# Retention and softplus feed-forward on one core: all attention in double steps of 64x64 products

## The chip, the core and the metric

The kernel runs on one core of one Trainium2 chip. Time is device time in microseconds, the median of repeated runs. The engines that matter are TensorE (PE, with its weight loads as PEld), VectorE (DVE), ScalarE (ACT), GpSimd (POOL) and SyncE (SP), which issues the DMAs.

## The reference

```python
scores = scale * np.matmul(q, k.transpose(0, 1, 3, 2))        # batch 8, heads 8, 576 positions, 64 dims
gamma = 1.0 - 2.0 ** (-5.0 - np.arange(H, dtype=np.float32))  # one decay for each head
Dmat = np.where(rel >= 0, gamma[:, None, None] ** rel[None, :, :], 0.0)
attn = np.matmul(scores * Dmat, v)                            # retention: causal, no softmax
x = attn.transpose(0, 2, 1, 3).reshape(B * S, H * D)          # 4608 tokens x 512
h = x @ w_in                                                  # 512 x 2048
g = np.maximum(h, 0.0) + np.log1p(np.exp(-np.abs(h)))         # softplus
out = g @ w_out                                               # 2048 x 512
```

All inputs and the output are float32; the weights `w_in` and `w_out` are read as 64-bit words.

## The kernel before

**Feed-forward.** The 4608 tokens form 9 units of 512. Each unit passes 16 slots, one for each 128 columns of the hidden layer: 144 slots. In slot i, `hidden_mm` (L391) makes 128 hidden features of 512 tokens with 12 products of 512 columns, and `output_mm` (L423) adds the slot before into four output banks with 12 more. Both use numbers split into a rounded head and a rest (`HI`, `LO`), three products for each exact one (`TERMS`). Between the two stand `logs` (three ACT operations, L399 to L401), `softplus` (DVE, L405) and `softplus_split` (ACT L409, DVE L410).

**Weights.** They come as 32 pieces of 512 KB, two for each slot of the first unit, through three staging buffers, and are converted in four parts: `weight_a` (ACT L455, DVE L457), `weight_b` (DVE L463), `weight_c` (ACT L471) and `weight_d` (DVE L476). Three pieces (`START_WEIGHTS`) are taken up before the first slot; slot i converts pieces 3 + 2i and 4 + 2i, and finishes the one before.

**Attention.** The tokens are also cut into 36 chunks of 128; there are 4 pairs of heads. Retention in chunks needs, for each head: scores k.q inside the chunk under a causal mask, the values times these scores, the state (the sum of k v over earlier chunks, decayed) times q, and the new state. A batch element is 4.5 chunks long, so it begins at the start or in the middle of a chunk (`_chunk_kind`): there a mask and a cleared part of k keep the two apart. There are two ways to do it:

- *Double steps*, for the first 9 chunks, 18 in all: two pairs of heads at once, in plain float32. Scores are 4 products with 64 rows and 128 columns (L163), the state 4 with 64 columns (L168), the values 4 of 128 rows into 64 outputs (L205), the state times q 4 of 64x64 with 128 columns (L211). Each such product appears as two PE records. In L211 both row groups of the array write to one PSUM bank. Nine double steps (`AHEAD`) run in an opening before the first slot, the others one in every second slot.
- *Split steps*, for the other 27 chunks, 108 in all, one in each slot from slot 19: one pair of heads, whose operands POOL scales (L252, L257), ACT and DVE split into head and rest (L266 to L268), and PE multiplies in 9 products of 256 columns (L277, L286, L359). Scores are added and masked and split again by ACT, DVE and POOL (L295 to L329), states likewise (L316 to L340). ACT and DVE write the result into the tokens (`value_out`, L372 and L376).

**Order.** It is written out by hand: each engine runs its instructions in the order of the program, and an instruction that waits holds what is behind it on its engine. All loads and stores are issued on SP's one queue: raw q, k, v of a step (`load_double` and `load_upto`), weights, constants and outputs. A load waits for its buffer. In an opening iteration m, the scores of step m come first on PE, then the values of step m - 1. In a slot, the attention's products stand ahead of the hidden product.

Of the kernel before, what the change touches and what calls it, by code (L numbers as in the profile page):

```python
# [23 lines left out]
NSTEP = NCHUNK * NPAIR  # L24
# [3 lines left out]
STEPS = CPU * NPAIR  # L28
# [3 lines left out]
PCHUNK = 9  # L32
NDOUBLE = PCHUNK * NPAIR // 2
AHEAD = STEPS // 2 + 1
NPLAIN = PCHUNK * NPAIR
LEAD = NPLAIN - 2 * (NDOUBLE - AHEAD) - 1
PIECE = 512
VCOLS = slice(3 * C, 4 * C)
START_WEIGHTS = 3
OPENING = 5  # L40
OPEN = (6 * C + H + NPAIR, 6 * C)
RAWS = 2
# [18 lines left out]
def retention_softplus_ffn(ctx: ExitStack, tc, opening, first, others, w, dec, vsc, gchp, out):  # L61
# [10 lines left out]
    ps_y = ctx.enter_context(tc.tile_pool(name="ps_y", bufs=1, space=PSUM, side="right"))  # L72
    ps_h = ctx.enter_context(tc.tile_pool(name="ps_h", bufs=2, space=PSUM, side="right"))


    plain_pools, weight_pools = ExitStack(), ExitStack()
    ps_att = plain_pools.enter_context(tc.tile_pool(name="ps_att", bufs=1, space=PSUM))
    rawp = plain_pools.enter_context(tc.tile_pool(name="rawp", bufs=2))
    pconst = plain_pools.enter_context(tc.tile_pool(name="pconst", bufs=1))
    wst = weight_pools.enter_context(tc.tile_pool(name="wst", bufs=WBUFS, side="right"))  # L80
    later = {}

    vsc_sb = const.tile([P, H], F32, name="vsc_sb")
    gchp_sb = const.tile([P, NPAIR], F32, name="gchp_sb")


    parts = [pconst.tile([P, n], F32, name=f"part{i}") for i, n in enumerate(OPEN)]
    decp_sb = [x[:, 4 * C:6 * C].rearrange("p (s c) -> p s c", s=2) for x in parts]
    vscp_sb = parts[0][:, 6 * C:6 * C + H]
    gchp0_sb = parts[0][:, 6 * C + H:6 * C + H + NPAIR]  # L90
    mask = pconst.tile([P, C], F32, name="mask")
    mask2 = pconst.tile([P, C], F32, name="mask2")
# [15 lines left out]
    def load_double(m):  # L108

        if m == 0:  # L110
            at = 0
            for x in parts:
                nc.sync.dma_start(x, opening[:, at:at + x.shape[1]])
                at += x.shape[1]
            kq, kv = (x[:, 0:4 * C] for x in parts)
        elif m == 5:
            kq, kv = (moe.tile([P, 4 * C], F32, tag="ab", name="raw_ab") for _ in range(2))
            for i, x in enumerate((kq, kv)):
                nc.sync.dma_start(x, first[m - 1][:, 4 * C * i:4 * C * (i + 1)])
        else:  # L120
            pool, tag = (moe, "g") if m in (3, 4, 8) else (rawp, "rawp")
            r = pool.tile([P, 8 * C], F32, tag=tag, name=f"raw_{tag}")
            nc.sync.dma_start(r, first[m - 1])
            kq, kv = r[:, 0:4 * C], r[:, 4 * C:8 * C]
        kq, kv = (x.rearrange("p (a s c) -> p a s c", a=2, s=2) for x in (kq, kv))
        live[-1 - m] = dict(k=kq[:, 0], q=kq[:, 1], kp=kv[:, 0], v=kv[:, 1])
# [3 lines left out]
    def scale_next():  # L130


        m = scaled[0]
        if -1 - m not in live:
            return
        scaled[0] += 1
        L = live[-1 - m]
        half = m % 2
        nc.gpsimd.tensor_mul(L["q"], L["q"], decp_sb[half])
        start = _chunk_kind(m // 2)[0]  # L140
        if start:
            nc.gpsimd.memset(L["kp"][0:start], 0.0)
        if m >= AHEAD:
            v, f = value_scale(m)
            nc.gpsimd.tensor_mul(v, v, f.unsqueeze(2).broadcast_to([P, 4, D]))

    def value_scale(m):
        return live[-1 - m]["v"].rearrange("p s (h d) -> p (s h) d", h=2), vscp_sb[:, 4 * (m % 2):4 * (m % 2) + 4]
# [8 lines left out]
    def scores_double(m, banks):  # L157

        L = live[-1 - m]
        for s in range(2):  # L160
            for h in range(2):
                rows = slice(h * D, (h + 1) * D)
                nc.tensor.matmul(banks[h][:, s * C:(s + 1) * C], L["k"][rows, s], L["q"][rows, s], start=True, stop=True)  # L163
        if _chunk_kind(m // 2)[1]:
            for s in range(2):
                for h in range(2):
                    rows = slice(h * D, (h + 1) * D)
                    nc.tensor.matmul(banks[0][rows, 2 * C + s * D:2 * C + (s + 1) * D], L["kp"][:, s, rows],  # L168
                                     L["v"][:, s, rows], start=True, stop=True, skip_group_check=True)
        L["banks"] = banks  # L170

    def scores_double_out(m):
        L = live[-1 - m]
        start, follows = _chunk_kind(m // 2)
        a = moe.tile([P, 2, 2, C], F32, tag="osb", name="a2")
        msk = mask2 if start else mask
        for h in range(2):
            nc.vector.tensor_mul(a[:, h], L["banks"][h][:, 0:2 * C].rearrange("p (s c) -> p s c", s=2),  # L178
                                 msk.unsqueeze(1).broadcast_to([P, 2, C]))
        L["a"] = a  # L180
        L["before"] = states.get(m % 2)
        states[m % 2] = None
        if follows:
            st = L["banks"][0][:, 2 * C:3 * C].rearrange("p (s d) -> p s d", s=2)
            s = att.tile([P, 2, D], F32, tag="s", name="s2", bufs=NPAIR + 1)
            if start is None:
                nc.vector.tensor_add(s, st, L["before"])
            else:
                nc.vector.tensor_copy(s, st)
            half = m % 2  # L190
            nc.gpsimd.tensor_mul(s, s, gchp0_sb[:, 2 * half:2 * half + 2].unsqueeze(2).broadcast_to([P, 2, D]))
            states[m % 2] = s

    def values_double(m, banks):

        L = live[-1 - m]
        start, _ = _chunk_kind(m // 2)
        n_cross = C if start is None else start
        if L["before"] is None:
            n_cross = 0  # L200
        o = [b[:, VCOLS] for b in banks]
        for s in range(2):
            for h in range(2):
                rows = slice(h * D, (h + 1) * D)
                nc.tensor.matmul(o[s][rows], L["v"][:, s, rows], L["a"][:, h, s], start=True,  # L205
                                 stop=not n_cross, skip_group_check=True)
        if n_cross:
            for s in range(2):
                for h in range(2):
                    rows = slice(h * D, (h + 1) * D)  # L210
                    nc.tensor.matmul(o[s][rows, 0:n_cross], L["before"][rows, s], L["q"][rows, s, 0:n_cross],  # L211
                                     start=False, stop=True, skip_group_check=True)
        L["o"] = o

    def values_double_out(m, both=None):
# [480 lines left out]
```

## Time and profile before

| | |
|---|---|
| median of 3 runs | 950.91 us (950.89 to 951.14) |
| profiled execution | 951.72 us, its span 950.0 us |
| mean granted TensorE clock | 0.999 |
| PE busy | 941.0 us, 99% of the span, 4946 records |
| DVE, ACT busy | 663.9 us (70%), 676.0 us (71%) |
| POOL busy | 274.8 us (29%) |
| bytes moved | 79.86 MB |

A PE record is busy from its start to a modelled end, and records overlap, so PE's share of 99% says that it always had something in hand, not that the array was full. The length of a piece of PE work is read from the start of one group to the start of the next. `x8` counts records; idle time in square brackets stands in front of the group and names what ended it.

### The profile page before, as it was taken

The numbers are of one execution on the slowest core, as the hardware profiler recorded it, in microseconds if no ns is written. First come the engines' busy times: TensorE is split into PE (matmuls) and PEld (weight loads), VectorE is DVE, ScalarE is ACT, GpSimd is POOL, SyncE is SP. The second block draws the span as 40 slices with busy tenths as digits, with TensorE's granted clock in tenths as the row PEclk, the third lists the DMA queues.
The fourth block names the chain that finished last, engine by engine and source line by source line (L and its number), as shares of the span: only waits on it lengthen the run. The fifth ranks groups of instructions, "written<-read, shape, count | busy, mean of one in ns | idle before, by whom it ended". The sixth has DMA issues, their size and how long they took to land.

```text
span 950.0 us, 14542 instructions
## 1 busy us (share of the span) xinstructions
PE 941.0 (99%) x4946; PEld 789.0 (83%) x4946; DVE 663.9 (70%) x1511; ACT 676.0 (71%) x1453; POOL 274.8 (29%) x497
## 2 busy tenths in 40 slices
PE   8999999999999999999999999999999999999998
PEld 6777778888888888888888888888888888888886
DVE  6777856777877787777777787777777777753222
ACT  7586756777777787777777787777777777764444
POOL 5111113333333332333343333233333333310000
PEclk9999999999999999999999999999999999999999
DMA  8666531222312222223212222223212222201001
GB/s 303 200 193 203 187 135 50 67 58 60 111 53 65 67 95 67 67 58 104 67 53 65 67 95 68 67 57 105 67 51 66 72 90 67 67 1 45 1 1 45
DMA packets 28730, 79.86 MB, mean 84 GB/s; under 512 B 3440, under 2 KB 3440, under 8 KB 28656
## 3 DMA queue, kind: packets, MB, share of 16 engines
q1 hardware_dynamic: 28656, 78.93, 26.6%
q8 instruction: 39, 0.64, 0.3%
q14 instruction: 35, 0.29, 0.1%
HBM read 69.48 MB, written 9.44 MB: 83 GB/s over the span
## 4 chain that ended last, share of the span: by engine, by line
PE 91%; ACT 4%; DVE 3%; DMA 1%; issue 1%; POOL 0%; DVEq 0%; ACTq 0%; POOLq 0%
PE h L391 39%; PE y L423 38%; PE os L359 6%; PE sc L277 3%; PE os L286 2%; DMA wst<-w 1%; DVE g L410 1%; DVE ab L405 1%; ACT w L471 1%; ACT ab L400 1%; ACT ab L401 1%; DVE wst L463 1%; DVE a L178 1%; ACT wst L455 1%; PE idle L512 0%
## 5 line engine op out<-in xcount | busy, mean ns | idle before, releaser
L391 PE MATMUL h<-xt,w 128*128 128x512 f32 (+1 forms) x1740 | 419.7, 390 | 1.2 <-DVE w L476 1.2
L423 PE MATMUL y<-w,g 128*128 128x512 f32 x1728 | 416.1, 390 | 0.6 <-DVE g L410 0.6
L423 PEld LDWEIGHTS y<-w,g 128*128 128x128 f32 x1728 | 323.9, 188 | 70.0 <-DVE g L410 2.9
L391 PEld LDWEIGHTS h<-xt,w 128*128 128x128 f32 x1740 | 317.6, 189 | 63.4 <-DVE w L476 2.7
L252 POOL TENSOR_TENSOR raw<-raw,dec_sb 128x256 f32<-128x256 f32 x108 | 96.4, 893 | 429.0 <-DMA raw<-others 381.2
L410 DVE TENSOR_TENSOR g<-ab,g 128x512 fp32r<-128x512 f32 (+1 forms) x145 | 103.4, 713 | 87.3 <-ACT g L409 86.2
L405 DVE SCALAR_TENSOR_TENSOR ab<-h,ab 128x512 f32<-128x512 f32 (+1 forms) x145 | 99.8, 688 | 90.1 <-ACT ab L401 87.5
L409 ACT CAST g<-ab 128x512 fp32r<-128x512 f32 (+1 forms) x145 | 89.5, 617 | 98.7 <-DVE ab L405 97.5
L399 ACT ACTIVATE ab<-h 128x512 f32<-128x512 f32 (+1 forms) x145 | 86.3, 595 | 72.0 <-PE h L391 72.0
L401 ACT ACTIVATE ab<-ab 128x512 f32<-128x512 f32 (+1 forms) x145 | 91.3, 630 | 4.7
L400 ACT ACTIVATE ab<-ab 128x512 f32<-128x512 f32 (+1 forms) x145 | 91.2, 629 | 4.6
L266 ACT CAST hl<-raw 128x768 fp32r<-128x768 f32 x108 | 90.9, 842 | 0.0
L296 DVE TENSOR_TENSOR a<-sc,a 128x256 f32<-128x256 f32 x108 | 45.9, 425 | 60.2 <-ACT a L295 60.0
L372 ACT CAST xt<-os 64x128 fp32r<-64x128 f32 x216 | 56.3, 260 | 44.1 <-PE os L286 40.0
L268 DVE TENSOR_TENSOR hl<-raw,hl 128x512 fp32r<-128x512 f32 x108 | 84.8, 785 | 1.5
L359 PE MATMUL os<-ah,hl 128*128 128x256 f32 x324 | 72.8, 285 | 0.0
L376 DVE TENSOR_TENSOR xt<-os,xt 64x128 fp32r<-64x128 f32 x216 | 62.2, 288 | 2.8
L320 POOL TENSOR_TENSOR s<-s,gchp_sb 128x128 f32<-128x128 f32 x96 | 59.3, 618 | 10.5 <-DVE s L319 0.4
L359 PEld LDWEIGHTS os<-ah,hl 128*128 128x128 f32 x324 | 53.3, 191 | 0.1
L297 POOL TENSOR_SCALAR_AFFINE_SELECT a<-a 128x256 f32<-128x256 f32 x108 | 44.1, 409 | 28.5 <-DVE a L296 26.6
L267 DVE TENSOR_TENSOR hl<-raw,hl 64x256 fp32r<-64x256 f32 x108 | 46.0, 426 | 6.7 <-ACT hl L266 3.7
L328 ACT CAST ah<-a 128x256 fp32r<-128x256 f32 x108 | 44.0, 407 | 7.9 <-POOL a L297 4.9
(101 smaller groups left out, 777.5 us busy)
## 6 DMA issues: line engine op xcount, KB each, us to landing
raw<-others SPq DMA_DIRECT2D x108, 384.0 KB, 3.1
wst<-w SPq DMA_DIRECT2D x32, 512.0 KB, 3.7
out<-osb SPq DMA_DIRECT2D x34, 256.0 KB, 2.3
raw_rawp<-first SPq DMA_DIRECT2D x13, 512.0 KB, 4.9
raw_g<-first SPq DMA_DIRECT2D x3, 512.0 KB, 7.3
raw_ab<-first SPq DMA_DIRECT2D x2, 256.0 KB, 8.4
dec_sb<-dec SPq DMA_DIRECT2D x1, 512.0 KB, 3.8
out<-part SPq DMA_DIRECT2D x2, 256.0 KB, 2.4
```

The source lines that it names most:

```text
L252: nc.gpsimd.tensor_mul(r[:, 2:4], r[:, 2:4], later["dec"][:, 2 * pr:2 * pr + 2])
L266: nc.scalar.copy(hl[:, 0:6], r)
L268: nc.vector.tensor_sub(hl[:, 6:10], r[:, 2:6], hl[:, 2:6].bitcast(F32))
L359: nc.tensor.matmul(o[:, :, 0:width], lhs, rhs, start=(n == 0), stop=(n == len(mms) - 1))
L391: nc.tensor.matmul(h, ws[p][:, a, kt * P:(kt + 1) * P], xt[:, b, kt, cols], start=(n == 0), stop=(n == 3 * NKT - 1))
L399: nc.scalar.activation(ab, h, AF.Abs)
L400: nc.scalar.activation(ab, ab, AF.Exp, scale=-1.0)
L401: nc.scalar.activation(ab, ab, AF.Ln, bias=1.0)
L405: nc.vector.scalar_tensor_tensor(ab, h, 0.0, ab, op0=ALU.max, op1=ALU.add)
L409: nc.scalar.copy(g[:, HI], ab)
L410: nc.vector.tensor_sub(g[:, LO], ab, g[:, HI].bitcast(F32))
L423: nc.tensor.matmul(y, g[:, a, at:at + P], ws[p][:, b, PIECE:], start=(p == 0 and n == 0), stop=(p == NF - 1 and n == 2))
```

## The change

All 36 chunks are now done in double steps, 72 of them, and the split steps are gone with everything that served them: their buffers and PSUM banks, the splits, `load_upto`, `scale_step`, `split_step`, `scores_mm`, `state_mm`, `value_mm`, `value_out` and their outputs. A double step itself is new. A chunk is cut into two halves of 64, with a state between them. Scores are then taken inside a half only, and what a half needs of earlier positions comes from the state before it: the chunk's first half from `before`, the second from `between`. As batch elements begin at multiples of 64, no mask or cleared k is needed for their starts.

Every product is 64x64 with 64 columns. In each group of four, the four pairs (t, h) name the four quarters of the array, and row group r always writes to bank r:

```diff
+    quads = [(t, h) for t in range(2) for h in range(2)]
...
+        for s in range(2):
+            for t, h in quads:
+                nc.tensor.matmul(bank[rows[t], h, SCOLS][:, part[s]], L["k"][rows[h], s, part[t]],
+                                 L["q"][rows[h], s, part[t]], start=True, stop=True, skip_group_check=True)
+        for s in range(2):
+            for t, h in quads:
+                if follows if t else start != HC:
+                    nc.tensor.matmul(bank[rows[h], t, TCOLS][:, part[s]], L["kp"][rows[t], s, rows[h]],
+                                     L["v"][rows[t], s, rows[h]], start=True, stop=True, skip_group_check=True)
...
+    def values(m, banks):
...
+        for s in range(2):
+            for t, h in quads:
+                nc.tensor.matmul(o[t][rows[h], part[s]], L["v"][rows[t], s, rows[h]], L["a"][rows[t], h, s],
+                                 start=(s == 0), stop=L["states"][t] is None, skip_group_check=True)
+        for s in range(2):
+            for t, h in quads:
+                if L["states"][t] is None:
+                    continue
+                if t == h:
+                    lhs, rhs = L["states"][t], L["q"][rows[t], s, part[t]]
+                else:
+                    lhs, rhs = L["sx"], L["q"][rows[t], s, C:QC]
+                nc.tensor.matmul(o[t][rows[h], part[s]], lhs[rows[t], s], rhs, start=False, stop=True,
+                                 skip_group_check=True)
```

For the quarters off the diagonal, the operands must stand on the other 64 partitions: q is loaded a second time for them (`crossed`, 64 more columns a pair), and the states are put into `sx`:

```diff
+        nc.vector.tensor_mul(a.rearrange("p h s c -> p (h s) c"),
+                             bank[:, :, SCOLS].rearrange("p h (s c) -> p h s c", s=2),
+                             mask.unsqueeze(1).broadcast_to([P, 4, HC]))
...
+        if before is not None:
+            nc.gpsimd.tensor_copy(sx[rows[0]], before[rows[1]])
+        if start != HC:
+            between = att.tile([P, 2, D], F32, tag="u", name="u")
...
+                nc.vector.tensor_add(between, sums[0], before)
+                nc.vector.tensor_add(sx[rows[1]], sums[0][rows[0]], before[rows[0]])
...
+                nc.vector.tensor_add(s, sums[1], between)
```

The step's raw tile has 1152 columns (576 KB) in place of 1024, and POOL's scaling of q covers 384 columns in place of 256. Around the step: `START_WEIGHTS` is 2; the raw tiles have three buffers; the opening keeps nine steps with their own PSUM banks, which the output banks take over after it; and each odd slot up to 127 has one double step, with ACT's copy of the values ahead of DVE's scores on the program's order:

```diff
     for i in range(NSLOT):
+        m = AHEAD + (i - 1) // 2
+        if i % 2 and m <= NSTEP:
+            both = ps_att.tile([P, 2, 4 * C], F32, tag="bank", name="bank")
+            scores(m, both)
+            values(m - 1, [both[:, n] for n in range(2)])
+            rest = values_out(m - 1, both)
+            scores_out(m)
             rest()
+            load_next()
+            scale_next()
         if i == NSLOT - 1:
             break
+        n = START_WEIGHTS + 2 * i
+        weight_a(n)
+        weight_cd(n - 1)
+        weight_b(n)
         h = hidden_mm(i)
         ab = logs(h)
+        softplus(h, ab)
+        weight_cd(n)
+        gs[i] = [softplus_split(ab)]
+        weight_a(n + 1)
+        weight_b(n + 1)
```

The hidden products, the softplus, the output products and the tail after slot 127 stay as they are; all output rows now go out through four buffers of their own.

More of the change, by code (lines that the diff above doesn't have):

```diff
@@ L60, in retention_softplus_ffn @@
 @with_exitstack
-def retention_softplus_ffn(ctx: ExitStack, tc, opening, first, others, w, dec, vsc, gchp, out):
+def retention_softplus_ffn(ctx: ExitStack, tc, first, others, consts, w, out):
     nc = tc.nc
@@ L172, in scores_double_out, with scores @@
-    def scores_double_out(m):
-        L = live[-1 - m]
-        start, follows = _chunk_kind(m // 2)
[L175 to L179, printed above, removed]
-        L["a"] = a
-        L["before"] = states.get(m % 2)
+    def scores(m, bank):
+        if m >= NSTEP:
+            return
+        L = live[m]
+        start, follows = _chunk_kind(m // 2)
+        for s in range(2):
+            for t, h in quads:
[6 more added lines that the diff above has]
+                                     L["v"][rows[t], s, rows[h]], start=True, stop=True, skip_group_check=True)
+        L["bank"] = bank
@@ L182, in scores_double_out @@
         states[m % 2] = None
         if follows:
[L184 to L187, printed above, removed]
+            s = att.tile([P, 2, D], F32, tag="s", name="s", bufs=4)
+            if between is None:
+                nc.vector.tensor_copy(s, sums[1])
             else:
-                nc.vector.tensor_copy(s, st)
+                nc.vector.tensor_add(s, sums[1], between)
@@ L190, in scores_double_out @@
             half = m % 2
-            nc.gpsimd.tensor_mul(s, s, gchp0_sb[:, 2 * half:2 * half + 2].unsqueeze(2).broadcast_to([P, 2, D]))
+            nc.gpsimd.tensor_mul(s, s, gchp[:, 2 * half:2 * half + 2].unsqueeze(2).broadcast_to([P, 2, D]))
             states[m % 2] = s
[L194 to L200, printed above, removed]
+    def values(m, banks):
+        L = live[m]
@@ L271, in scores_mm @@
-    def scores_mm(j):
-        if not ok(j):
-            return
-        L = live[j]
-        sc = later["ps_sc"].tile([P, 2, 2, C], F32, tag="sc", name="sc")
-        for h in range(2):
-            nc.tensor.matmul(sc[:, h], L["hl"][:, h], L["hl"][:, 2 + h:7 + h:4], start=True, stop=True)
-        L["sc"] = sc
-    def state_mm(j, bank):
-        if not ok(j) or not _chunk_kind(steps[j][0])[1]:
-            return
-        L = live[j]
-        st = bank[:, 2 * C:4 * C].rearrange("p (a d) -> p a d", a=2)
-        for n, part in enumerate((8, 4)):
-            nc.tensor.matmul(st, L["hl"][:, part], L["hl"][:, 5:10:4], start=(n == 0), stop=(n == 1))
-        L["st"] = st
@@ L428, in output_out @@
         y = ys[u][tt]
-        if u == 0 and tt > 1:
-            osb = parts[tt - 2][:, 0:DM]
-        else:
-            osb = (later["osb"] if tt > 1 else moe).tile([P, DM], F32, tag="osb", name="osb")
+        osb = later["osb"].tile([P, DM], F32, tag="osb", name="osb")
         if tt % 2 == last:
@@ L516, in retention_softplus_ffn @@
     for m in range(AHEAD):
-        pair = [ps_y.tile([P, 4 * C], F32, tag=f"y{2 * (m % 2) + h}", name="pair") for h in range(2)]
+        pair = ps_open.tile([P, 2, 4 * C], F32, tag="pair", name="pair")
         if m % 2:
             both, vbanks = None, [ps_h.tile([P, 4 * C], F32, tag="h", name="hv") for _ in range(2)]
-        else:
-            both = bank() if m else None
-            vbanks = m and halves(both)
+        elif m:
+            both = ps_att.tile([P, 2, 4 * C], F32, tag="bank", name="bank")
+            vbanks = [both[:, n] for n in range(2)]
@@ L629, in retention_softplus_ffn @@
-        if ends:
-            output_out(i // NF - 1, 3)
+            if i % NF == 0:
+                for tt in range(CPU):
+                    output_out(i // NF - 1, tt)
     hs = [hidden_mm(i, slice(n, n + T // 2)) for n in (0, T // 2)]
```

438 lines of the change are left out of this document (122 added, 316 removed).

## The prediction, made before the change was run

> **What bounds the kernel now.** I read the page first, then the busy times by stage, then the TensorE timeline and the chain of waits inside the stages.
>
> ```profile
> PE 941.0 (99%) x4946; PEld 789.0 (83%) x4946; DVE 663.9 (70%) x1511; ACT 676.0 (71%) x1453; POOL 274.8 (29%) x497
> PEclk9999999999999999999999999999999999999999
> PE 91%; ACT 4%; DVE 3%; DMA 1%; issue 1%; POOL 0%; DVEq 0%; ACTq 0%; POOLq 0%
> ```
>
> TensorE runs 99% of the span at full granted clock and holds 91% of the chain that ends last. The span falls into four stages, cut at the first hidden product, at that of slot 16 and at that of the last slot:
>
> ```profile
> 0.00:24.04 24.04, 21.33 (x266) 16.09 (x266) 15.38 (x45) 17.25 (x56) 12.63 (x26) 1.00 0.82 303
> 24.04:130.22 106.18, 104.30 (x624) 80.85 (x621) 81.80 (x153) 74.45 (x129) 15.22 (x25) 1.00 0.61 189
> ...
> 937.12:950.01 12.89, 8.51 (x49) 7.20 (x47) 3.73 (x8) 4.93 (x11) 0.00 (x0) 0.93 0.22 83
> ...
> 130.22:937.12 806.90, 806.90 (x4013) 684.89 (x4012) 562.97 (x1307) 579.38 (x1258) 246.94 (x446) 1.00 0.21 64
> ```
>
> Columns: length, then busy time of PE, weight loads, DVE, ACT, POOL, clock, DMA share, GB/s. The long third stage is busy without a gap on PE, while DVE and ACT have 30% to spare there. So only PE time counts in it. In the second (weight) stage ACT and DVE stand near 75% and the slots lean on them too. The opening is shared by DMA (82%) and PE.
>
> What a slot costs on PE, with one split attention step in it and without, and a double step:
>
> ```profile
> 200.75 0.40 PE L277 MATMUL sc<-hl 128*128 128x256 f32 x2
> ...
> 201.82 1.55 PE L391 MATMUL h<-xt,w 128*128 128x512 f32 x6
> ...
> 866.40 2.88 PE L391 MATMUL h<-xt,w 128*128 128x512 f32 x12
> ...
> 871.84 2.88 PE L391 MATMUL h<-xt,w 128*128 128x512 f32 x12
> ```
>
> ```profile
> 109.65 0.65 PE bank L163 x8
> 110.30 0.38 PE bank L168 x8
> 110.68 0.44 PE bank L205 x8
> 111.12 0.58 PE bank L211 x8
> 111.70 2.94 PE h L391 x12
> 114.65 2.72 PE y L423 x12
> 117.37 2.72 PE h L391 x12
> 120.09 2.82 PE y L423 x12
> 122.91 0.65 PE bank L163 x8
> ```
>
> The first rows are the PE timeline, the second the chain of waits. A bare slot is 871.84 - 866.40 = 5.44 us. A split step holds PE from 200.75 to 201.82, 1.07 us, so two of them, which do a double step's work, 2.14. Today's double step is 0.65 + 0.38 + 0.44 + 0.58 = 2.05 us. Around it the product before takes 2.82 and the one after 2.94 where the plain ones take 2.72: another 0.32 for going into and out of the small-tile forms, 2.37 in all. Today's double step is no cheaper than two split ones; everything hangs on what the new one costs.
>
> **The change part by part.**
>
> *The new double step on PE.* It has 8 products for the scores, 8 for the half-chunk states, 8 for values and 8 across: 32 of 64x64 with 64 columns, two records each, 64 records. Four different tiles of the array follow one another in the program, so it is 16 groups of four records if the four run together. No row of before has four together, but line 211 on a short chunk has the new record's exact shape, with two tiles. The same PE rows, asked for up to 28.67, 28.69, 28.75 and 28.94 us, and then the next product:
>
> ```profile
> 28.57 0.27 PE L211 MATMUL bank<-raw_g,s 64*64 64x64 f32 x2
> ...
> 28.57 0.33 PE L211 MATMUL bank<-raw_g,s 64*64 64x64 f32 x4
> ...
> 28.57 0.39 PE L211 MATMUL bank<-raw_g,s 64*64 64x64 f32 x6
> ...
> 28.57 0.45 PE L211 MATMUL bank<-raw_g,s 64*64 64x64 f32 x8
> ...
> 28.95 0.50 PE L391 MATMUL h<-xt,w 128*128 128x512 f32 x1
> ```
>
> The records begin two at a time: two by 28.67, four by 28.69, six by 28.75. So two tiles overlap, and a pair costs some 0.06 us. Eight records take 28.95 - 28.57 = 0.38, of which 4 x 0.06 are pairs and 0.14 is entry and exit. As a check, the 128-column form above takes 0.58 for its eight: 0.20 more for four pairs, 0.05 per 64 columns. The lines 163 and 168 make pairs of the other two kinds (two row groups to two banks, two column halves of all rows), and also run eight records in 0.65 and 0.38.
>
> The bounds for a group of four are then 0.05 (column time alone) and 0.12 (two pairs after each other). I take 0.06: the new tiles use the row overlap of line 163 and the column overlap of line 168, each of which is there, and the four write four different halves of banks. A full step is 0.14 + 16 x 0.06 + 0.32 = 1.42 us. Of nine chunks, three leave out products (no state at a start, none handed on at an end), 32 of 576, which makes the mean 0.46 + 15.1 x 0.06 = 1.37.
>
> *Third stage.* 127 bare slots are 127 x 5.44 = 690.9; steps stand in every second slot, from 17 to 127, 56 x 1.37 = 76.7. Sum 767.6 against 806.9: **-39.3 us**. Taken out with the split steps is work on the other engines:
>
> ```profile
> L266 ACT CAST hl<-raw 128x768 fp32r<-128x768 f32 x108 | 90.9, 842 | 0.0
> ...
> L178 DVE TENSOR_TENSOR a<-bank,mask 128x256 f32<-128x256 f32 x18 | 6.8, 417 | 0.7 <-DMA out<-osb 0.7
> ...
> L187 DVE TENSOR_TENSOR s<-bank,s 128x128 f32<-128x128 f32 x6 | 1.7, 282 | 0.0
> ```
>
> The 842 ns cast, its subtractions and the splits of scores and states go, and are worth nothing here, as PE's products cover them. What comes instead on DVE is one mask (417 ns) and three state sums (282), 1.26 us a double step, needed two slots later (10.9 us of products). Were that cover gone, 56 x 1.26 = 71 us would be lost; the two slots stand against it.
>
> *Weight stage.* The change starts with two pieces of weights ready in place of three, so the hidden product of slot i+1 now waits for the piece that slot i splits after its softplus. The chain of waits gives that loop:
>
> ```profile
> 44.21 2.96 PE h L391 x12
> ...
> 48.65 0.51 ACT ab L399
> ...
> 49.18 0.64 ACT ab L400
> ...
> 49.84 0.64 ACT ab L401
> ...
> 50.51 0.70 DVE ab L405
> ...
> 61.98 0.71 DVE w L476
> ```
>
> 2.96 + 0.51 + 0.64 + 0.64 + 0.70 + 0.71 = 6.16, with five hand-overs of some 0.02: 6.26 us. It decides in the slots without a step (5.44 bare) and in the first two; the slots with one are 5.44 + 1.42 = 6.86, set by PE. Of the 16 slots, 9 x 6.26 + 7 x 6.86 = 104.3 against 106.18: **-1.9 us**. What stands behind the waiting hidden product on PE is the output product of the slot before, whose operands are ready; nothing else waits for it. So the cheaper step pays little here. Left as it is, the loop would give back at most 0.8 us a slot.
>
> *Opening.* PE gets through faster, but POOL and DMA set the pace:
>
> ```profile
> 6.39 0.73 POOL L139 TENSOR_TENSOR raw_rawp<-raw_rawp,part 128x256 f32<-128x256 f32 x1 [1.66 <-DMA raw_rawp<-first]
> ...
> L191 POOL TENSOR_TENSOR s<-s,part 128x128 f32<-128x128 f32 x8 | 4.9, 618 | 4.3 <-DVE s L187 3.0 <-DVE s L189 1.3
> ...
> L493 POOL COPY mask<-mask 128x128 f32<-128x128 f32 x1 | 0.3, 289 | 0.1
> ```
>
> POOL scales 384 columns of q per step in place of 256, 0.73 x 1.5 = 1.1 us, scales the state (0.62) and now copies half a state across (up to 0.29): 2.0 us a step, nine steps 18 us from about 4.5 on, then the last scores. That ends near 23 us. A step's load also grows from 512 to 576 KB, and stands ahead of the weights on SP's queue. I take 23.3 against 24.04: **-0.7**; 21 to 26 is possible.
>
> ```profile
> raw<-others SPq DMA_DIRECT2D x108, 384.0 KB, 3.1
> wst<-w SPq DMA_DIRECT2D x32, 512.0 KB, 3.7
> raw_rawp<-first SPq DMA_DIRECT2D x13, 512.0 KB, 4.9
> ```
>
> After the opening a double step loads 576 KB in one DMA where two split steps load 768 in two; at 21% busy engines that is free. The load waits on SP for the values of the step before; behind it queue weight pieces and output stores. A piece that lands in 3.7 us has a slot of 6.3 to come, so this costs nothing unless that wait passes some 2.5 us.
>
> *Sum.* 23.3 + 104.3 + 767.6 + 12.9 (the tail, untouched) = 908.1 against the span of 950.0. The profiled execution took 951.72, 1.72 over its span; the median 950.91 lies 0.81 below that. So 908.1 + 0.9 = **909 us**.
>
> **The rivals.**
>
> *No more than two tiles at a time* (slower). The place is the double step in the third stage: if four tiles run as two pairs, it is 30.2 x 0.06 + 0.46 = 2.27 on the mean, 690.9 + 56 x 2.27 = 818.0, and the weight stage 9 x 6.26 + 7 x 7.82 = 111.1. With 23.3 and 12.9 that makes 965.3, **966 us**. For it: no row shows more than two. Against it: pairs exist along rows and along columns, so nothing in the rows serializes either direction. It turns from gain to loss where 23.3 + 56.3 + 7 x 5.44 + 690.9 + 12.9 + 60.8 steps = 950, at 2.11 us a step: 0.103 us a group, 26 ns a record.
>
> *A floor per record.* No row shows records coming faster on the mean than the pairs above at their lower bound, 0.05 us for two, 25 ns each; it may be a pace of the engine and not of the columns. Then a group is 0.10, the mean step 1.97, the third stage 801.2, the weight stage 108.8: 946.2, **947 us**, hardly faster. Against it: the two records of a pair start within 0.02 us (two at 28.67, four at 28.69). The Trainium skill, "TensorE: Matmul & The Clock Gate", section "Wait — 56ns, not 53.3ns?", states such a floor: start to start never below about 25 ns, however few the columns. The rows speak against it for two different tiles, and none shows a long run.
>
> *Instruction supply.* A step has 128 PE instructions (a load with each record) where two split steps have 36. Today's step gets 64 through in 2.05 us, 32 ns each; at that rate the new one takes 4.1 and the kernel loses over 100 us. Line 168 passes 16 in 0.38, so I hold it unlikely; at that 24 ns a step would be 3.1 + 0.3 and the time near 1,030.
>
> *The gain is lost in the weight stage.* If one piece less in hand lets pieces arrive late, slots of 7.8 us (today's with a step) would come in all 16: 125 in place of 104, **930 us**.
>
> **How the numbers follow.** Forecast 70%, two tiles 12%, floor 7%, weight stage 7%, supply 4%. The likeliest alone has 895 to 925: 0.05 a group gives 9 us less, opening and loop some 3 to 5 either way. A measurement of this kernel tells 0.2%, 1.9 us, from no change. Forecast, weight stage and most of the floor are faster: 81%; the rest of the floor is the same: 4%; two tiles, supply and what I have not thought of are slower: 15%. The range 895 to 950 holds forecast, weight stage and floor, 8 in 10 or a little more; leaving out the 966.
>
> **What would show it.** After: PE records of 64x64 in groups of four within some 0.06 us and 1.1 us from the first score product to the hidden product; slots of 6.8 and 5.5 us in turn after slot 17; the same 5.44 at the end. In the weight stage the hidden product waits for DVE's weight subtraction in slots without a step. In the opening POOL is nearly without gaps. I am wrong if the records come in pairs, if gaps open within the step, or if the third stage shows PE idle, which would mean that a state or a mask comes late.

## The result

The changed kernel takes **918.6 us** (918.09 to 920.91) against 950.95 us (950.89 to 951.14) before: ratio 0.9664, 95% interval 0.9647 to 0.9681. The forecast of 909 us was 9.6 us too low, inside its range. The sign and the place of the gain came as worked out; one term, the opening, was missed by 9.9 us, about as much as the whole time.

The page of the changed kernel, busy times and granted clock, and its instruction queue:

```profile
PE 890.4 (97%) x7830; PEld 725.7 (79%) x7830; DVE 375.6 (41%) x745; ACT 442.1 (48%) x775; POOL 165.6 (18%) x270
...
PEclk7899999999999999999999999999999999999999
...
q8 instruction: 61, 1.00, 0.5%
```

TensorE has 58% more records and 51 us less to do; DVE and ACT lost a third of their work and more, which is worth nothing by itself. The clock line is new: it starts below 9, where that of before was 9 throughout. The last row (packets, MB, share) is taken up below.

The stages of the changed kernel, cut as before (length, then PE, weight loads, DVE, ACT, POOL, clock, DMA share, GB/s):

```profile
0.00:33.19 33.19, 19.42 (x531) 16.62 (x531) 15.15 (x48) 15.21 (x52) 17.93 (x34) 0.79 0.78 273
33.19:140.55 107.36, 98.71 (x854) 77.87 (x853) 90.52 (x164) 78.75 (x133) 24.91 (x34) 0.98 0.55 182
140.55:904.34 763.79, 763.79 (x6402) 624.04 (x6400) 266.19 (x528) 343.22 (x580) 122.78 (x204) 1.00 0.16 53
904.34:916.60 12.26, 8.50 (x49) 7.19 (x47) 3.72 (x8) 4.94 (x11) 0.00 (x0) 1.00 0.23 86
```

| stage | before | forecast | after | missed by |
|---|---|---|---|---|
| opening | 24.04 | 23.3 | 33.19 | +9.9 |
| weight stage | 106.18 | 104.3 | 107.36 | +3.1 |
| third stage | 806.90 | 767.6 | 763.79 | -3.8 |
| tail | 12.89 | 12.9 | 12.26 | -0.6 |

The third stage gave 43.1 us, PE still without a gap in it. The opening gave 9.2 of them back: PE was idle there for 24.04 - 21.33 = 2.7 us before and for 33.19 - 19.42 = 13.8 us now.

The chain of waits through one double step of the third stage:

```profile
204.43 2.72 PE y L280 x12
207.15 0.39 PE bank L150 x16
207.54 0.23 PE bank L155 x16
207.77 0.23 PE bank L204 x16
208.00 0.23 PE bank L214 x16
208.24 2.95 PE h L248 x12
```

Sixteen records in 0.23 us are four groups of four at 0.058 us. The step holds 1.09 us, and the product behind it takes 0.23 more than a plain one: 1.32 us in all against 2.37 before. Slots follow each other at 6.62 and 5.58 us, which is 12.20 - 2 x 5.44 = 1.32 again.

What PE waits for in the opening, from the list of waits (us in total, times, longest):

```profile
PE bank L214 <- POOL sx L177: 5.8, 3, 3.7
PE pair L150 <- POOL raw_rawp L127: 2.7, 1, 2.7
PE hv L214 <- POOL sx L177: 2.1, 2, 1.2
...
PE bank L204 <- DVE xt L233: 1.0, 1, 1.0
```

The place of the longest of them in the timeline of POOL and PE:

```profile
29.74 0.99 POOL L127 TENSOR_TENSOR raw_rawp<-raw_rawp,consts_sb 128x384 f32<-128x384 f32 x1 [3.32 <-DMA raw_rawp<-others]
30.69 0.61 POOL L130 TENSOR_TENSOR raw_rawp<-raw_rawp,consts_sb 128x256 f32<-128x256 f32 x1
31.36 0.29 POOL L177 COPY sx<-s 64x128 f32<-64x128 f32 x1
...
31.70 0.37 PE L214 MATMUL bank<-raw_rawp,sx 64*64 64x64 f32 x2 [3.68 <-POOL sx L177]
```

PE waits for a copy of 0.29 us of step 7's state. The copy stands in POOL's queue behind the scaling of step 9's queries, and that waits for step 9's load. In the order of the program the scaling of a later step comes first.

### The profile page after: what moved, and what is told of

It reads as the page before. It is cut to its first block, busy times and chain, and to the rows that moved or that the text cites. A ratio compares the mean times of both kernels' runs of the same rounds, so it can differ in the third digit from the quotient of the medians.

```text
span 916.6 us, 18132 instructions
## 1 busy us (share of the span) xinstructions
PE 890.4 (97%) x7830; PEld 725.7 (79%) x7830; DVE 375.6 (41%) x745; ACT 442.1 (48%) x775; POOL 165.6 (18%) x270
## 4 chain that ended last, share of the span: by engine, by line
PE 90%; DVE 3%; ACT 3%; DMA 2%; POOL 1%; issue 0%; SPq 0%; POOLq 0%; DVEq 0%
PE h L248 43%; PE y L280 40%; PE bank L150 3%; PE bank L214 2%; PE bank L204 2%; PE bank L155 1%; DMA raw_g<-others 1%; DVE w L330 1%; DMA raw_rawp<-others 1%; DVE ab L262 1%; ACT ab L257 1%; ACT ab L258 1%; DMA wst<-w 1%; DVE wst L317 1%; ACT w L325 0%; ACT ab L256 0%
## 5 line engine op out<-in xcount | busy, mean ns | idle before, releaser
L127 POOL TENSOR_TENSOR raw_rawp<-raw_rawp,consts_sb 128x384 f32<-128x384 f32 x69 | 72.1, 1045 | 198.8 <-DMA raw_rawp<-others 195.6
L195 POOL TENSOR_TENSOR s<-s,consts_sb 128x128 f32<-128x128 f32 x64 | 26.1, 408 | 417.8 <-DVE s L193 368.6
L130 POOL TENSOR_TENSOR raw_rawp<-raw_rawp,consts_sb 128x256 f32<-128x256 f32 x63 | 41.7, 661 | 0.0
L229 ACT CAST xt<-bank 128x256 fp32r<-128x256 f32 x68 | 25.4, 373 | 32.8 <-PE bank L214 32.8
L214 PE MATMUL bank<-raw_rawp,sx 64*64 64x64 f32 x472 | 27.8, 221 | 4.1 <-POOL sx L177 4.1
L204 PE MATMUL bank<-a,raw_rawp 64*64 64x64 f32 x1056 | 30.1, 221 | 1.0 <-DVE xt L233 1.0
L233 DVE TENSOR_TENSOR xt<-bank,xt 128x256 fp32r<-128x256 f32 x68 | 28.3, 416 | 6.5 <-ACT xt L229 6.3
L168 DVE TENSOR_TENSOR a<-bank,mask 128x256 f32<-128x256 f32 x63 | 26.6, 423 | 9.6 <-ACT xt L229 9.6
L150 PE MATMUL bank<-raw_rawp 64*64 64x64 f32 x1008 | 29.1, 230 | 0.0
L177 POOL COPY sx<-s 64x128 f32<-64x128 f32 x64 | 24.8, 388 | 8.8 <-PE bank L214 4.8
L155 PE MATMUL bank<-raw_rawp 64*64 64x64 f32 x888 | 25.9, 218 | 0.0
```

The lines of the kernel that those rows point to most:

```text
L127: nc.gpsimd.tensor_mul(q, q, decq[m % 2])
L150: nc.tensor.matmul(bank[rows[t], h, SCOLS][:, part[s]], L["k"][rows[h], s, part[t]], L["q"][rows[h], s, part[t]], start=True, stop=True, s ...
L204: nc.tensor.matmul(o[t][rows[h], part[s]], L["v"][rows[t], s, rows[h]], L["a"][rows[t], h, s], start=(s == 0), stop=L["states"][t] is None ...
L214: nc.tensor.matmul(o[t][rows[h], part[s]], lhs[rows[t], s], rhs, start=False, stop=True, skip_group_check=True)
```

## The experiments

Times are medians; ratios are to the kernel before on the same chip.

### The opening: POOL's order

```diff
         scale_values(m + 1)
-        scale_next()
         scores_out(m)
...
         if m == 8:
             weight_a(1)
+        scale_next()
```

> The changed kernel, with POOL's scaling of the step after next put at the end of each opening iteration (behind the copy of the half state) as the kernel before had it. Theory A, POOL's order: in the opening the copy into sx for step 7 stands behind the scaling of step 9, whose load lands at 29.58 us, and PE waits 3.68 us for it; without that the first hidden product starts near 29 in place of 33.2 us, PE's waits for POOL's copy (8 us in five places) fall under 2, and the time falls by about 4 us, to 914 or 915. Theory B, the loads' pace sets the opening whatever POOL does: first hidden product at 32 or later, 917 or more.

915.54 us, 0.9605 (0.9586 to 0.9623). Its opening and weight stage by windows:

```profile
0.00:29.44 29.44, 18.34 (x530) 15.88 (x531) 15.04 (x47) 14.94 (x52) 15.27 (x30) 0.77 0.81 288
29.44:138.07 108.63, 100.04 (x854) 78.83 (x853) 90.40 (x164) 78.97 (x134) 27.77 (x37) 0.97 0.57 185
```

Its list of waits of PE in the opening:

```profile
PE pair L150 <- POOL raw_rawp L127: 4.0, 2, 3.0
PE pair L150 <- POOL s L195: 3.6, 1, 3.6
...
PE hv L214 <- issue: 0.7, 1, 0.7
```

The waits for `sx` are gone and the first hidden product comes 3.75 us earlier. So POOL's order cost that much, shown. But the weight stage grew by 1.3 us, and 6.1 us of the missed 9.9 remain, with a wait of 3.6 us in a new place.

### The opening: four short loads for step 0

```diff
-            for to, at in ((consts_sb, slice(0, SMALL + H + NPAIR)), (r, slice(0, KQ)), (r, slice(KQ, RAW)),
-                           (consts_sb, slice(NCONST - SMALL, NCONST))):
-                nc.sync.dma_start(to[:, at], (first if to is r else consts)[:, at])
+            nc.sync.dma_start(consts_sb, consts)
+            nc.sync.dma_start(r, first)
```

> The changed kernel, with step 0 and the constants loaded by two DMAs in place of four (constants first, then the whole raw tile). Theory B, the loads' pace: step 1's scaling starts near 7.5 us in place of 9.6 and the opening ends 2 us earlier, so 916.5. Theory A, POOL's order and the late load of step 9: the early gain is taken back at the wait for step 9 unless that load is issued earlier too; within 0.5 us of the changed kernel, 918.

918.42 us, 0.9640 (0.9624 to 0.9656): no change. Step 1 is scaled at 8.41 us in place of 9.62, step 0 at 6.97 in place of 4.81, the first hidden product comes at 32.79 in place of 33.19. As long as POOL's order stands, how step 0 is loaded changes nothing. With that order mended it was not tried, although PE's wait of 2.6 to 3.0 us for step 1's scaled queries (0.7 at most in the kernel before) is in every later version.

### The weight stage: three pieces ready

```diff
-START_WEIGHTS = 2
+START_WEIGHTS = 3
...
-        if m == 8:
+        if m == 7:
             weight_a(1)
-    weight_b(1)
+        if m == 8:
+            weight_b(1)
+            weight_cd(1)
+            weight_a(2)
+    weight_b(2)
```

> The changed kernel with three pieces of weights converted before the first slot, as before, in place of two. Theory L, the loop hidden product - logs - softplus - weight subtraction - next hidden product sets the slots without a step: these fall from 6.4 to 6.5 us to about 5.6, the weight stage from 107.4 to about 100, PE's wait for the weight subtraction (8.6 us) goes, and the time falls to 911 or 912. Rival M, ACT and DVE are simply full in this stage (DVE 90.5 of 107.4 us): slots as they are, change under 1 us, 918.

915.93 us, 0.9616 (0.9602 to 0.9631). Its weight stage by windows:

```profile
33.23:138.34 105.11, 100.63 (x854) 77.78 (x853) 91.76 (x163) 77.50 (x132) 25.07 (x35) 0.98 0.56 186
```

Most slots without a step fall to 5.58 us, as PE alone would have them (the others take 5.9 and 6.6), but most of those with one rise to 7.5 to 7.9: from slot 2 on, two slots take 13.2 us on the mean, as with two pieces (13.2). The gain of 2.3 us, between theory L's 7 and rival M's under 1, comes from the first two slots. The loop through the softplus, which the prediction charged, no longer sets the slots without a step here, and the pair of slots is no shorter. DVE is busy for 91.76 of 105.11 us, which points at its conversion of the weights; this run does not show it.

### The third stage: in what order four tiles come

First the two quarters on the diagonal of the array for a whole product, then the two off it:

```diff
+    pairs = [((0, 0), (1, 1)), ((0, 1), (1, 0))]
+    ordered = [(s, t, h) for pair in pairs for s in range(2) for t, h in pair]
```

> The changed kernel with the same 32 products of a step in another order: each four groups first on the two tiles of the diagonal, then on the two others, so that only two tiles follow one another. Theory F, the gain is four tiles at a time and PE keeps the program's order: a section of eight records on two tiles takes twice as long, a step goes from 1.09 us to about 2.0, and the time rises by 56 x 0.93 + 7 us, to 970 to 978. Rival R, PE draws the other two tiles' records forward, or the gain has another source than four at a time: the step stays near 1.1 us and the time near 918; half way (940 to 955) if its look-ahead covers part of a section.

923.64 us, 0.9698 (0.9677 to 0.9719). Its chain, end of a step (the pieces of under 0.06 us between them are records that start together):

```profile
208.37 0.23 PE bank L215 x14
208.60 2.96 PE h L249 x12
```

Fourteen records still pass in 0.23 us, four abreast, although the program now names eight records of two tiles before the eight of the other two. The step takes 1.14 us in place of 1.09, and the whole kernel some 3 to 6 us more than the changed one (0.9698 against its 0.9664 and, in a later comparison, 0.9636). PE takes records of a free tile ahead of records that wait for a busy one: in this step's timeline the ninth and the eleventh record of the last section (the first that read `sx`) start at 208.20 us, beside the second and the fourth.

Then all products of one tile (16 records) before the next tile's:

```diff
-            scores(m, both)
-            values(m - 1, [both[:, n] for n in range(2)])
+            by_tile(m, both)
```

> In the slots every product of a step is issued tile by tile: all of one 64x64 tile's scores, state, values and across products (16 records), then the next tile's. Nothing else changes. Theory F (the gain of the third stage comes from four tiles running at once; the PE looks only so far ahead, some 16 to 18 records by the diagonal-first order): with 16 records of one tile in a row at most two tiles overlap, and a step in a slot takes between twice and four times its 1.09 us, 1.9 to 3.7 us by the spacing of the chain's rows; 64 steps then add 50 to 165 us: 965 to 1,080 us. Rival L (the PE draws any tile's records forward, however far back they stand): the step stays at 1.1 to 1.2 us and the time at 916 to 924 us.

1047.78 us, 1.1011 (1.0993 to 1.1029). Its third stage by windows:

```profile
153.62:1032.57 878.95, 878.95 (x6402) 737.35 (x6400) 265.74 (x528) 343.95 (x580) 120.11 (x204) 1.00 0.14 46
```

Its chain of waits at the end of one step:

```profile
203.90 0.23 PE bank L174 x4
204.13 0.23 PE bank L177 x4
204.37 0.23 PE bank L186 x4
204.60 2.99 PE h L278 x12
```

One tile alone needs 0.23 us for four records: 0.058 each, as much as a group of four tiles. The same 64 records now cost (878.95 - 127 x 5.44) / 56 = 3.36 us a step; the changed kernel's own by that sum is 1.30. That is the value of four tiles at once: 2.06 us a step, 115 us in this stage, shown by undoing it alone. PE's view ahead is short: it mends the order of eight records, and little of sixteen, where the first record of a tile starts only beside the fourth-last of the tile before.

An order with both row groups writing to one PSUM bank was not tried, so what the separate banks are worth stays open.

### The opening again: more loads up front

Steps 5 to 7 go into the second token buffer, idle until the first slots; POOL's order as in the first experiment. (Lines in this kernel and the next stand 5 further down.)

```diff
+        if m in (5, 6, 7):
+            if m == 5:
+                later["x"] = xpool.tile([P, 2, NKT, T], F32, tag="xt", name="raw_x")
+            r = later["x"].rearrange("p a k t -> p (a k t)")[:, (m - 5) * RAW:(m - 4) * RAW]
...
-    for m in range(5):
+    for m in range(8):
         load_step(m)
```

> The scaling at the end of each opening iteration as in the run before, and steps 5 to 7 loaded up front into the second token buffer, which is idle until the first slots, so that no load of the opening waits for a buffer. Theory A (the opening's excess over the forecast is loads that wait for buffers, then POOL's order; what is left is POOL's 2.0 us a step): the first hidden product comes at 24 to 26 us instead of 29.4. If the weight stage keeps its 108.6 us, the time is 911 to 912 us. Rival M (the weights' conversion on DVE and ACT sets the pace from the first slot, and its pieces come no earlier): the weight stage grows by what the opening loses, and the time stays at 914 to 916 us.

915.5 us, 0.9618 (0.9603 to 0.9632): no faster than with five loads. The first hidden product comes at 29.99 us; theory A is wrong. The time is rival M's, but not for its reason: the opening lost nothing, and the weight stage kept its length (108.51 against 108.63 in the first experiment). Loads that wait for buffers were not what was left. The timeline shows something else:

```profile
15.80 0.27 PE L155 MATMUL pair<-raw_g 64*64 64x64 f32 x1
18.08 0.40 PE L155 MATMUL pair<-raw_g 64*64 64x64 f32 x12 [2.00 <-issue]
```

PE stops for 2.00 us in the middle of the same line, and the instruction behind the gap carries no wait that the profile shows ("issue"). The DMA view of this stretch alone, 15.7 to 18.1 us:

```profile
q1 hardware_dynamic: 229, 0.95, 98.1%
q8 instruction: 1, 0.02, 2.8%
```

One packet of instructions passes in it, from 15.72 to 16.80, between loads that fill the DMA engines. Over the whole run the page counts 61 such packets of 16 KB for 7830 records, some 128 a packet; the page of the kernel before has 39 for 4946:

```profile
q8 instruction: 39, 0.64, 0.3%
```

So PE's instructions come in blocks of 128 records with their weight loads, two double steps, and in the opening PE uses a block up in 2.2 to 5 us. The first experiment's 3.6 us fits the same reading. The list names POOL's `s` for it, which had ended at 22.24 + 0.40 = 22.64; PE resumed at 23.63, by that kernel's timeline:

```profile
22.24 0.40 POOL L195 TENSOR_TENSOR s<-s,consts_sb 128x128 f32<-128x128 f32 x1
...
23.63 0.70 PE L150 MATMUL pair<-raw_rawp 64*64 64x64 f32 x16 [3.56 <-POOL s L195]
```

None of the four semaphores that PE takes there rose after 22.65; PE took the first at 23.42. At least 0.8 us belong to nothing that it waits for.

### Both gains together

The eight loads with three pieces of weights.

> The same with three weight pieces converted in the opening instead of two. If both gains add (opening 24 to 27 us, weight stage 105 us, third stage 763.8, tail 12.3): 906 to 909 us. If the third piece's conversion on DVE and ACT delays the opening by as much as it saves later: 911 to 914 us.

912.26 us, 0.9587 (0.9572 to 0.9601); opening 29.55 us, weight stage 104.50. The third piece's gain held, and the eight loads had none to add. The time lies in the second range of the expectation, but not for its reason: the third piece did not delay the opening (29.55 against 29.99).

### POOL beside DVE

In the changed kernel's timeline, the same operations of DVE without and with POOL's scaling beside them:

```profile
67.63 0.69 DVE L267 TENSOR_TENSOR g<-ab,g 128x512 fp32r<-128x512 f32 x1
68.24 0.42 DVE L311 TENSOR_SCALAR wst<-wst 128x512 int32<-128x512 uint32 x1
...
73.64 1.54 POOL L127 TENSOR_TENSOR raw_rawp<-raw_rawp,consts_sb 128x384 f32<-128x384 f32 x1 [2.47 <-DMA raw_rawp<-others]
...
74.40 1.33 DVE L267 TENSOR_TENSOR g<-ab,g 128x512 fp32r<-128x512 f32 x1
75.65 0.83 DVE L311 TENSOR_SCALAR wst<-wst 128x512 int32<-128x512 uint32 x1
```

Both engines take longer: 1.33 for 0.69, 0.83 for 0.42 (beside POOL's next operation, from 75.14 to 76.21), and POOL 1.54 for the 0.99 of the opening. The price of it, by leaving POOL's scaling out for seven steps of this stage, so that their queries and values stay unscaled:

```diff
             load_next()
-            scale_next()
+            if i < NF - 1:
+                scaled[0] += 1
+            else:
+                scale_next()
```

> The run with eight loads and three pieces, with POOL's scaling of queries and values left out for the seven steps that POOL scales in the weight stage (this part of the computation is left out, so it is a price and not a version). Theory P (POOL's scaling overlaps DVE's work and lengthens it: in the after trace DVE's g subtraction takes 1.08 and 1.33 us where it overlaps POOL's scaling and 0.69 us elsewhere, the piece's scaling 0.51 to 0.83 against 0.42, and DVE is busy 88 to 90% of this stage): the weight stage shortens by 0.7 to 0.9 us a step, 5 to 6 us in all, to 99 to 100 us. Rival (DVE has slack enough, and ACT or the loads set the pace): the stage shortens by less than 1.5 us.

The weight stage goes from 104.50 to 101.92 us (909.68 us, 0.9558, 0.9544 to 0.9572). The stage with the scaling, by windows:

```profile
29.55:134.05 104.50, 99.45 (x854) 77.57 (x853) 90.86 (x163) 77.56 (x132) 26.94 (x37) 0.98 0.56 187
```

And without it:

```profile
30.84:132.76 101.92, 99.30 (x853) 77.91 (x853) 84.57 (x163) 76.75 (x132) 9.93 (x20) 0.98 0.58 192
```

DVE's busy time falls by 6.3 us, as theory P had it, the stage by 2.6 only: neither bound held. The overlap lengthens DVE's work as expected (the mean of its `g` subtraction falls from 881 to 689 ns without it, that of the weights' subtraction from 766 to 720), but DVE is not alone in setting the pace: its idle time ahead of the weights' subtraction, which ACT's copy ends, grew from 4.2 to 6.3 us.

### Where the instructions go: fewer loads ahead

```diff
-        if m == 3:
+        if m == 5:
             load_weight(0)
...
-        if m in (1, 2, 3):
+        if m in (3, 6, 7):
             load_next()
-        if m in (3, 4):
-            load_weight(m - 2)
+        if m in (2, 6):
+            load_weight(1 + m // 4)
```

> The kernel with eight loads and three pieces, its loads in another order: the first weight piece after step 5 instead of step 3, steps 8 to 10 and the third piece only when the opening is at steps 3, 6 and 7, so that fewer loads stand in front of the DMA engines while the opening runs. Theory I (PE runs dry: its instructions come in packets of 16 KB, 128 records each, and in the opening a packet starts 3.6 to 3.9 us after PE begins the block before it, behind the loads, against 1.1 us where the engines are idle; PE resumes 1.3 to 1.8 us after the packet's end): PE's gap of 4.24 us before the third of these blocks shrinks to 1 to 2 us, the first hidden product comes at 26.5 to 28 us instead of 29.55, and if the weight stage keeps its 104.5 us the time is 909.5 to 911 us. Rival B (PE waits for POOL's copy, as the list of waits has it): the gap stays at 3.5 to 4.2 us, the first hidden at 29 to 30, the time at 912 us. The weights' later loads can lengthen the weight stage in both cases.

913.03 us, 0.9585 (0.9571 to 0.9599), first hidden product at 30.67 us, later than either side expected. The stand, as such a stop of PE is called from here on, in its timeline:

```profile
23.68 0.71 PE L155 MATMUL pair<-raw_x 64*64 64x64 f32 x16 [4.24 <-POOL sx L182]
```

The stand is 4.24 us, to the hundredth the one without this edit, and the packet starts 3.55 us into the block, against 3.62: rival B's number. So what delays a packet is not those later loads; that part of theory I fell. The opening is 1.1 us longer than without the edit, with a new stand of 1.20 us at record 472 (records are counted from PE's first). That PE waits for POOL's `sx` doesn't follow: the first semaphore that PE takes there is DVE's, raised at 22.38 and taken at 23.46, a good 1 us later and before the copy ended at 23.52.

The same, with the values' scaling on ACT in the weight stage:

```diff
-        if m >= AHEAD:
+        if m >= AHEAD + 8:
             v, f = value_scale(m)
...
             rest()
+            scale_values(m + 1)
             load_next()
```

> The same, and in the weight stage the scaling of the values moves from POOL (one operation of 0.97 to 1.06 us) to ACT (four of 0.27 us), as the opening has it. Theory P (POOL's work beside DVE's lengthens both; leaving out 2.0 us of it a step took 2.6 us off the stage): half of POOL's scaling gone from 8 steps, 1 to 1.5 us off the weight stage. Rival (ACT is as scarce as DVE there): no change or up to 2 us longer.

911.91 us, 0.9568 (0.9552 to 0.9584), the weight stage 103.25 in place of 104.13: 0.9 us, somewhat under theory P's bound. The intervals of the two overlap.

The changed kernel itself, beside these two:

> The changed kernel itself, on the same chip as the two beside it: 918 to 920 us, first hidden product at 33 us.

917.92 us, 0.9636 (0.9622 to 0.9650), first hidden product at 32.71 us.

Last, 64 records put where PE idles, so that the blocks' boundaries move by one step:

```diff
+    ahead = [idle, ps_h.tile([P, T], F32, tag="h", name="idle")]
+    for n in range(8):
+        for t, h in quads:
+            nc.tensor.matmul(ahead[h][rows[t], 256:272], fill[rows[h], rows[t]], fill[rows[h], 0:16],
+                             start=True, stop=True, skip_group_check=True)
     scale_next()
```

> The kernel with the values scaled by ACT, with 32 small matmuls on a constant (64 records, half a packet of instructions) put in front of step 0, where PE idles; nothing reads them. Theory I (PE runs dry between packets: in the kernel without them it stands for 1.18 us after record 219 and 4.24 us after record 346, and at 346 every semaphore that it waits for was up over 1 us earlier): each packet's boundary moves one step earlier, and the third packet is asked for while PE waits for step 1's load anyway; the stand after 219 goes, the one before step 6's scores moves or shrinks to under 2 us, and the first hidden product comes at 28 to 29.5 us instead of 30.99; time 909 to 911 us. Rival B (PE waits there for POOL or for a load): the stand of 4.2 us stays before step 6's scores, the first hidden product at 30.7 to 32 us, the time at 912 to 913 us.

910.43 us, 0.9565 (0.9549 to 0.9581); first hidden product at 29.41 us in place of 30.99. PE's list of waits in the opening without them:

```profile
PE pair L155 <- POOL sx L182: 4.2, 1, 4.2
...
PE hv L219 <- issue: 1.2, 1, 1.2
PE pair L155 <- issue: 1.2, 1, 1.2
```

And with them:

```profile
PE pair L155 <- POOL s L200: 2.4, 1, 2.4
PE bank L219 <- issue: 1.6, 1, 1.6
...
PE pair L155 <- issue: 0.4, 1, 0.4
```

Theory I's forecast: the stand after record 219 shrank from 1.19 to 0.39 us, the one after 346 is still after record 346, which is now one step earlier in the work, and shorter (2.41); the third, at record 472 or 473, was 1.20 and is 1.62. Adding work to PE made the opening 1.6 us shorter than without it, which brings it back to the level of the kernel with eight loads and three pieces (29.55). The granted clock was no higher with the added records: 0.56 and 0.71 from 8 to 16 and from 16 to 24 us, against 0.57 and 0.89. Nor is it POOL's copy that PE had waited for: the copy that the list names, at 23.55 to 23.84 us without the records, now comes at 25.12, and step 6's scores start at 22.21 without it. That PE's stands go with the count of its records, and not with a step's data, is shown. The expectation said too much in one point: at record 346 POOL's semaphore last rose at 23.85, just before PE went on at 23.99; only the others had been up for over 1 us. The times of stands and packets, from the trace:

```
kernel                   PE stands        packet           PE resumes after its end
scaling last             20.07 to 23.63   20.99 to 21.92   1.71
eight loads              16.07 to 18.08   15.72 to 16.80   1.28
eight loads              21.27 to 24.78   21.98 to 23.06   1.72
eight loads, three       19.50 to 23.73   20.91 to 21.98   1.75
loads in turn            19.44 to 23.68   20.79 to 21.82   1.86
values on ACT            19.75 to 23.99   21.22 to 22.30   1.69
records ahead            18.82 to 21.23   18.76 to 19.84   1.39
the changed kernel       26.45 to 27.46   25.03 to 25.96   1.50
```

The stands at records 219 and 472 of these kernels that are not listed give 1.3 to 1.5 us. In the kernel before, PE's list of waits in the opening has no stand of this kind: after the start it names only POOL's scaling, 1.2 us in all. What decides when a packet is asked for stays open.

The version with the values on ACT beats both kernels: 0.9568 (0.9552 to 0.9584) against 0.9636 (0.9622 to 0.9650) for the changed kernel in the same comparison. The last one was compared on another chip; its ratio, 0.9565, is no different from that.

## Why the prediction was right, and where not

- *The double step on PE.* Right. A group of four takes 0.058 us, where 0.06 was taken between 0.05 and 0.12. The full step costs 1.32 in place of 1.42: the 0.32 that the products around it lose was 0.23, while the step itself came as summed (1.09 against 0.14 + 0.96, with 0.16 of entry, 0.39 - 0.23). With 56 steps that is the third stage's -3.8 us. It hid as much of the other stages' misses, which is luck.
- *No more than two tiles at a time.* Wrong; two other orders gave 1.14 and 3.36 us a step, and the loss appears only when the program itself holds the tiles apart.
- *A floor per record.* It did not come: 16 records pass in 0.23 us, 14 ns each, and the 64 of a step in 0.39 + 3 x 0.23 = 1.08 us, 17 ns each with the entry. The Trainium skill, "TensorE: Matmul & The Clock Gate", section "Wait — 56ns, not 53.3ns?", has 25 ns as the least distance of two starts; this trace doesn't agree for four different tiles. For one tile 58 ns were measured.
- *Instruction supply.* The rival had the right resource, at a steady rate and in the wrong stage; what shows is blocks that come late. In the third stage PE never lacks instructions: 64 records and 64 loads pass in 1.09 us. In the opening, where the steps follow each other without the long products between them, it does.
- *Weight stage.* 104.3 against 107.36. Slots with a step came at 6.75 to 6.84 (6.86 forecast), those without at 6.36 to 6.53 (6.26) but for one of 7.17 and the last of 5.59, and the first two at 7.85 and 6.95. The sum also had one step too few: there are eight in this stage and not seven, which makes it 105.0. The loop through the softplus was the wrong bound: with it removed by a third piece, two slots still took 13.2 us. DVE's conversion, lengthened by POOL, was not in the sum; POOL's share of it is shown (2.6 us), the rest is argued from DVE's busy time. The rival of 930 us, slots of 7.8 throughout, did not come; only the first was one.
- *Opening.* This step failed: "POOL scales 384 columns of q per step ... 2.0 us a step, nine steps 18 us from about 4.5 on". POOL's work a step was sized nearly rightly (1.00 + 0.44 + 0.35 us against 1.1 + 0.62 + 0.29; that its 17.93 us busy equal the 18 is in part chance, as they hold the scaling of two more steps), but it was added up as if it ran without gaps. It is one link of a chain through POOL, DVE and PE, whose order, and not its length, decided: 3.75 us lay in POOL's order (shown by the first experiment). Of the remaining 6 us, a part lies in PE's instruction packets (moving them changed the opening by 1.6 us in the last experiment, whose stands still add up to 4.4 us). The wait for step 1 and the clock granted to PE may hold another part; neither was tried on its own. Windows of the changed kernel's opening, the clock third from the right:

```profile
0.00:8.00 8.00, 5.91 (x42) 4.30 (x42) 0.48 (x1) 2.35 (x5) 1.82 (x8) 1.00 0.71 222
8.00:16.00 8.00, 4.97 (x162) 4.78 (x162) 5.13 (x18) 4.97 (x19) 4.64 (x6) 0.57 0.89 331
16.00:24.00 8.00, 5.27 (x216) 4.81 (x220) 6.42 (x19) 5.32 (x20) 6.44 (x12) 0.79 0.94 327
```

In the kernel with eight loads, at a granted clock of 0.50 from 24 to 28 us, sixteen records take 0.43 us in its chain in place of 0.23, so a step costs some 0.8 us more there, an estimate from these two. The opening of before had 1.00. How the 6 us divide among these was not settled; no version brought the opening under 29.4 us.

- *The chances.* Those for slower, 15%, are less than those of two tiles and of supply together, 12 and 4.

## What to carry to other kernels

Sixty-four-row, sixty-four-column products in float32 pay when consecutive instructions go to four different tiles: the group costs what one does, and an order that stays on one tile for sixteen records loses all of it. When a change removes an engine's load, look at the order of the small operations that others wait for, and add up the chain and not the busy times. More instructions (here 58% more records) were free beside long products and not in a stretch of short ones: count records per step there.

## What had not been expected of the hardware

- PE starts records of a free tile ahead of earlier ones for a busy tile, so between tiles it does not keep the program's order: it went seven records ahead in the order by pairs, which cost 0.05 us a step, and only four in the order by tiles. What sets the reach stays open.
- A packet of 16 KB brings 128 records with their loads, takes about 1 us, and PE went on 1.3 to 1.9 us after its end where it had run dry. The Trainium skill, "Runtime: NRT & Kernel Launch", section "Instruction fetch mechanics", has blocks of this size, 256 instructions, fetched while the one before runs and mostly hidden. The runs agree on the size and, in the third stage, on the hiding; in the opening they don't, with stands of up to 4.2 us.
- POOL's scaling and DVE's work on SBUF lengthen each other, DVE by 0.41 and 0.64 us in the rows above. The Trainium skill, "SBUF — State Buffer", section "Who interferes with whom", gives a port that the two share; the rows agree, with both sides longer (1.54 for 0.99 us on POOL).
- PE's granted clock fell to 0.57 in a stretch in which PE was busy 4.97 of 8 us, and was 1.00 before it and in the third stage.
